# Thresholded attention feeding a leaky-ReLU layer pair: small threshold operations and some copies change engine, transposed weights change their PSUM banks and shape, and early loads change place

## The chip, the cores and the metric

The kernel runs on one core of one Trainium2 chip. The metric is device microseconds of one execution, taken as the median of several runs. The core has five engines that each work through their own list in order: PE (matrix multiply, with a list of weight loads beside it), DVE (VectorE), ACT (ScalarE), POOL (GpSimd) and SP, which here only issues DMAs. Engines wait for each other through semaphores.

## The reference

```
def _attn_ref(q, k, v, tau):                      # q, k, v: 8 batches, 8 heads, 576 positions, 64 wide
    scale = 1.0 / np.sqrt(q.shape[-1])
    scores = scale * np.matmul(q, k.transpose(0, 1, 3, 2))
    thresh = np.max(scores, axis=-1, keepdims=True) - tau          # tau = 0.02
    scores = np.where(scores >= thresh, scores, -1000000000.0)
    scores = scores - np.max(scores, axis=-1, keepdims=True)
    attn = np.exp(scores)
    attn = attn / (np.sum(attn, axis=-1, keepdims=True) + 1e-09)
    return np.matmul(attn, v)

def reference(...):
    x = attn_out.transpose(0, 2, 1, 3).reshape(4608, 512)
    h = x @ w_in                                  # w_in 512 x 2048
    g = np.maximum(0.01 * h, h)
    return g @ w_out                              # w_out 2048 x 512
```

## The kernel before

The work is a list of 144 steps, 18 for each of the 8 batches. A step has 128 query rows of two heads (a "pair" of heads, four pairs to a batch): first the 512 main positions as 16 steps (two blocks, four pairs, two halves `c`), then the 64 tail positions of all heads as two tail steps. The order of every engine's list is written out by hand: one loop over `n` (lines 479 to 516) emits, in this order, the parts of several steps at once.

For step `n` the parts are these. `scores` (L217) makes 12 matmuls into PSUM: q and k are each held as a high and a low fp16 half, and three products are summed. `copy_min` (L225) copies the scores from PSUM to `s` on DVE, negated and scaled, and accumulates the row minimum `mn`, once for each head. `threshold` (L231) adds tau to `mn` and gives `th`, a 128x2 tile; it is on POOL. `exps`, emitted one iteration later, runs on ACT: an exponential `e` for the first head (L253), and for the second head of a "steep" step a very steep Prelu against `th` (L249) and then the exponential with its sum (L250). A step is steep if `n` is below 12 or if nothing is transposed two iterations on. `weights` (L263) is the DVE counterpart: `w = (s <= th) * e` with its sum, for one head of a steep step and for both of another. `recip` (L269, DVE) and `widen` (L272, POOL) write the reciprocal of the sums into block 9 of `w`, so that it is transposed with the weights.

The transposed weights `wT` come from a DMA transpose on SP's queue (L280), except for the first eight steps (`early`), which are transposed on PE by `turn_w_pe` (L289), emitted two iterations after the step. It makes two groups of five transposes, each into a PSUM tile `wp`. Both tiles come from the ring with the tag `h`, which has two buffers. ACT copies the first group and DVE the second (L290). The second group holds block 9, so it needs `widen`. The ring `h` is shared with the tiles `tp` of the q and k transposes and with `hp` of the first layer. `pv` (L301) multiplies with v, and `evacuate` (L323, DVE) scales the result by the reciprocal and gives `x`.

q and k must be split and transposed first. The keys of batch 0 in order are k0, q0, the k tails, k1, q1, k2, q2, k3, q3 and the q tails. The first five are split by ACT and DVE (`split_now`, L158 and L159) and the others by three POOL operations each (`split_scale` L138, `split_high` L144, `split_low` L148). `turn` (L177) transposes a split key on PE in pieces of 64 columns, into `tp`; one copy (L188, or two of L180 for tails) brings it to `kT` or `qT`. This copy is on ACT unless the call names another engine. `turns_at`, `pool_at` and `loads_at` say which iteration emits which of these; the keys k2, q2, k3, q3 and the q tails are transposed in iterations 1, 2, 3, 4 and 8, and batch 1's from iteration 9 on.

The weights of the two layers are loaded as fp16 by DMAs on POOL's queue: four for `w_in` (L441), two after each of two early splits, and four for `w_out` (L444) in iterations 2 to 5. The other loads are on SP's queue, except q0 and q1 on ACT's. Once four pairs of a block are done, `layer1` (L344 on PE, Prelu L346 on ACT) and `layer2` (L357 on PE) are emitted, one unit of the first and two of the second to an iteration, which over a batch is just what the batch brings.

Iteration `n` thus puts on POOL: whatever `pool_at` holds, then `widen` of step `n-1`, then `threshold` of step `n`:

```
        for f in pool_at.get(n, []):
            f()
        if 1 <= n <= N:
            last = steps[n - 1]
            weights(last)
            ...                        # recip and widen of the last step
        if n < N:
            threshold(steps[n])
```

Of the kernel before, what the change touches and what calls it, by code (L numbers as in the profile page):

```python
# [10 lines left out]
FP16 = mybir.dt.float16  # L11
AX = mybir.AluOpType
# [26 lines left out]
def kernel(  # L39
# [10 lines left out]
    nc = tc.nc  # L50
# [4 lines left out]
    tau_f = float(tau)  # L55
# [4 lines left out]
    ps = ctx.enter_context(tc.tile_pool(name="ps", bufs=1, space=bass.MemoryType.PSUM))  # L60
# [3 lines left out]
    ident = sb.tile([128, 128], FP16, name="ident")  # L64
# [19 lines left out]
    def load_tails(b, which, eng=None):  # L84
        t = sb.tile([128, 2, 2, 64], FP32, tag="rawt", bufs=2, name="rawt")
        src = SRC[which][b, :, MAIN:S, :].rearrange("(u sh) p d -> u p sh d", u=2)
        for u in range(2):
            (eng or nc.sync).dma_start(out=t[ds(64 * u, 64), :, :, :].rearrange("p s h d -> p (s h) d"), in_=src[u])
        tails[b, which] = t
# [29 lines left out]
    def turned_of(b, which):  # L119
        if (b, which) not in turned:  # L120
            turned[b, which] = sb.tile([128, 2, NP, WIDE[which]], FP16, tag=f"{which}T", bufs=2, name=f"{which}T")
        return turned[b, which]
# [28 lines left out]
    def split_now(key):  # L151
        t = halves[key] = new_half()
        for i in range(2):
            if key[1] == "t":
                src, n = tails[key[0], key[2]][:, :, i, :], 2
            else:
                src, n = pair_of(*key)[:, i, :, :], 4
            nc.scalar.activation(out=t[:, 0, 0:n, i, :], in_=src, func=AF.Copy, bias=0.0, scale=64.0)  # L158
            nc.vector.scalar_tensor_tensor(out=t[:, 1, 0:n, i, :], in0=src, scalar=64.0, in1=t[:, 0, 0:n, i, :],  # L159
                                           op0=AX.mult, op1=AX.subtract)  # L160

    def turn(key, copy=None):
        copy = copy or nc.scalar.copy
        b, p, which = key
        dst, half = turned_of(b, which), halves.pop(key)
        n = 2 if p == "t" else 4
        c0 = 0 if which == "q" else 64
        if p == "t":
            c0 = MAIN if which == "q" else 0
            tp = ps.tile([128, 2, 2, 2, 64], FP16, tag="h", bufs=2, name="tp")  # L170
        else:
            tp = ps.tile([128, 2, 4, 128], FP16, tag="h", bufs=2, name="tp")
        for x in range(2):
            for t in range(n):
                for h in range(2):
                    o = tp[ds(64 * h, 64), x, :, t, :] if p == "t" else tp[ds(64 * h, 64), x, t, :]
                    nc.tensor.transpose(o, half[:, x, t, h, :], ident[:, :])  # L177
        if p == "t":
            for x in range(2):
                copy(out=dst[:, x, :, ds(c0, 64)], in_=tp[:, x, :, :, :].rearrange("d u s p -> d (u s) p"))  # L180
            if which == "k" and b:
                nc.gpsimd.tensor_copy(out=dst[:, :, :, 576:640], in_=dst[:, :, :, 0:64])
            elif which == "k":
                for x in range(2):
                    nc.vector.tensor_copy(out=dst[:, x, :, 576:640],
                                          in_=tp[:, x, :, :, :].rearrange("d u s p -> d (u s) p"))
        else:
            copy(out=dst[:, :, p, ds(c0, 512)], in_=tp[:, :, :, :].rearrange("d x t p -> d x (t p)"))  # L188
# [3 lines left out]
    steps = []  # L192
# [27 lines left out]
    def copy_min(st):  # L220

        st.mn = sb.tile([128, 2], FP32, tag="mn", bufs=3, name="mn")
        st.s = sb.tile([128, 2, 576], FP32, tag="s", bufs=2, name="s")
        for h in range(2):
            nc.vector.tensor_scalar(  # L225
                out=st.s[:, h, :].rearrange("p (a b) -> p a b", a=2), in0=st.sc[h][:, :, 0:288],
                scalar1=-1.0 / UNIT, scalar2=None, op0=AX.mult, op1=AX.min, accum_out=st.mn[:, h : h + 1])

    def threshold(st):
        st.th = sb.tile([128, 2], FP32, tag="th", bufs=3, name="th")  # L230
        nc.gpsimd.tensor_scalar(out=st.th[:, :], in0=st.mn[:, :], scalar1=1.0, scalar2=tau_f, op0=AX.mult, op1=AX.add)  # L231

    def exps(st):

# [32 lines left out]
    def recip(pr, c, n):  # L267
        pr.rec = sb.tile([128, 2, 2], FP32, tag="rec", bufs=2, name="rec")
        nc.vector.reciprocal(out=pr.rec[:, 0:n, :], in_=pr.sum[:, ds(c, n), :])  # L269
# [5 lines left out]
    def new_wt(pr):  # L275
        pr.wt = sb.tile([128, 2, 10, 128], FP16, tag="wT", bufs=4, name="wT")
# [6 lines left out]
    def turn_w_pe(pr, c):  # L283
        if c == 0:
            new_wt(pr)
        for half, copy in enumerate((nc.scalar.copy, nc.vector.tensor_copy)):
            wp = ps.tile([128, 5, 128], FP16, tag="h", bufs=2, name="wp")
            for i in range(5):
                nc.tensor.transpose(wp[:, i, :], pr.w[:, c, 5 * half + i, :], ident[:, :])  # L289
            copy(out=pr.wt[:, c, ds(5 * half, 5), :], in_=wp[:, :, :])  # L290

    def pv(st):
        st.pv = ps.tile([128, 4, 128], FP32, tag="pv", bufs=1, name="pv")
# [85 lines left out]
    loads_at, turns_at, pool_at = {}, {}, {}  # L379

    def at(d, n, f):
        d.setdefault(n, []).append(f)

    def units(b):
        u = [(b, p, w_) for p in range(NP) for w_ in "kq"]
        return u[:2] + [(b, "t", "k")] + u[2:] + [(b, "t", "q")]

    for b in range(1, B):
# [6 lines left out]
        for i, key in enumerate(units(b)):  # L395
            n_ = base + 4 + 18 * i // 10 if b > 1 else 9 + 3 * i // 2
# [19 lines left out]
    def load_pair(p, which, eng):  # L416
        if p % 2 == 0:
            raws[0, p // 2, which] = sb.tile([128, 4, 256], FP32, tag="raw", bufs=4, name="raw")
        eng.dma_start(out=raws[0, p // 2, which][:, ds(2 * (p % 2), 2), :],
                      in_=SRC[which][0, ds(2 * p, 2), 0:MAIN, :].rearrange("h (p t) d -> p h (t d)", t=4))  # L420
# [1 line left out]
    load_pair(0, "k", nc.sync)  # L422
    load_pair(0, "q", nc.scalar)
    load_tails(0, "k", nc.sync)
    load_pair(1, "q", nc.scalar)
    load_pair(1, "k", nc.sync)
    for p in (2, 3):
        load_pair(p, "k", nc.sync)
        load_pair(p, "q", nc.sync)
# [9 lines left out]
    def load_w(i):  # L439
        if i < 4:  # L440
            nc.gpsimd.dma_start(out=w_in16[:, i, :], in_=moe_w_in[ts(i, 128), :])  # L441
        else:
            j = i - 4
            nc.gpsimd.dma_start(out=w_out16[:, ds(4 * j, 4), :],  # L444
                                in_=moe_w_out[ds(512 * j, 512), :].rearrange("(j p) f -> p j f", p=128))

    for i in range(4):
        at(pool_at, 2 + i, lambda i=i: load_w(4 + i))

    def split_pool(key):  # L450
        split_scale(key)
        split_high(key)
        split_low(key)

    first = units(0)
# [4 lines left out]
    turn(first[2])  # L460
    for key in first[3:5]:
        split_now(key)
    for i, key in enumerate(first[5:7]):
        split_pool(key)
        load_w(2 * i)
        load_w(2 * i + 1)
    for n_, key in zip((0, 1, 6), first[7:]):
        at(pool_at, n_, lambda key=key: split_pool(key))
    at(turns_at, 0, lambda: turn(first[3]))
    at(turns_at, 0, lambda: turn(first[4], nc.vector.tensor_copy))  # L470
    for n_, key in zip((1, 2, 3, 4, 8), first[5:]):
        at(turns_at, n_, lambda key=key: turn(key))

    N = len(steps)
    for st in steps:
# [2 lines left out]
    n = 0  # L478
    while n < N + PV_LAG + 2 or l1q or l2q or stores:
        for f in loads_at.get(n, []):  # L480
            f()
        if 1 <= n <= N:
            exps(steps[n - 1])
        if n < N:
            scores(steps[n])
            copy_min(steps[n])
        if n - 1 in pv_at:
            evacuate(pv_at[n - 1], n)
        for f in pool_at.get(n, []):
            f()  # L490
        if 1 <= n <= N:
            last = steps[n - 1]
            weights(last)
            if last.early:
                recip(last.pair, last.c, 1)
                widen(last.pair, last.c, 1)
            elif last.tail or last.c == 1:
                recip(last.pair, 0, last.pair.n)
                widen(last.pair, 0, last.pair.n)
                turn_w(last.pair)  # L500
        if n < N:
            threshold(steps[n])
        while stores:
            store()
        if l1q and l1q[0][3] <= n:
            layer1()
        for f in turns_at.get(n, []):
            f()
        if 2 <= n < N + 2 and steps[n - 2].early:
            turn_w_pe(steps[n - 2].pair, steps[n - 2].c)  # L510
        for _ in range(2):
            if l2q:
                layer2()
        if n in pv_at:
            pv(pv_at[n])
        n += 1
# [33 lines left out]
```

## Time and profile before

| quantity | value |
|---|---|
| median of three runs | 531.41 us (530.39 to 531.99) |
| the profiled execution | 528.87 us, of which the span from first to last instruction is 527.1 us |
| busy share of the span: PE, DVE, ACT, POOL | 92%, 82%, 82%, 60% |
| PE busy from 160 to 475 us | 313.8 of 315 us |
| PE busy from 0 to 100 us | 70.7 of 100 us |
| start of the score copies of steps 0, 3, 8, 9, 13 and 19 (first L225 of the pair) | 12.65, 27.51, 45.10, 51.91, 62.55 and 84.65 us |
| mean granted TensorE clock | 0.983 |

The busy shares are averages over stages that differ. The last rows are the start of DVE's first score copy of a step, which serves as a clock of the loop: the first steps come slowly, and from about 160 us on PE is busy throughout. A span is measured from the first to the last instruction; the time of the profiled execution is 1.8 us longer.

### The profile page before, as it was taken

The page shows a single profiled execution, that of the slowest core. Times are in us where ns is not written, and L with a number is a line of the kernel's source. Part 1 is how long each engine was busy: PE and PEld are TensorE (multiplying, and loading weights), DVE is VectorE, ACT ScalarE, POOL GpSimd, SP SyncE. Part 2 cuts the span into 40 slices and gives each one's busy share as a digit, 9 for nine tenths or more (in the row PEclk, how much of TensorE's full clock was granted, in tenths as well). Part 3 has the DMA queues.
Part 4 walks back from the last instruction along what each step waited for, and adds up shares of the span by engine and source line. Part 5 has one row for each costly group of instructions (what it writes and reads, how often), then busy time and mean ns, then how long its engine had stood idle before and what let it go on. Part 6 is the DMA issues. An engine that isn't in the chain of part 4 may idle for free.

```text
span 527.1 us, 19148 instructions
## 1 busy us (share of the span) xinstructions
PE 487.0 (92%) x7824; PEld 343.5 (65%) x7824; DVE 432.7 (82%) x1182; ACT 431.3 (82%) x737; POOL 317.7 (60%) x559
## 2 busy tenths in 40 slices
PE   5586787998999999999999999999999999999995
PEld 3354565665766776676776676767767776667773
DVE  4577999999899988999899988998899988887100
ACT  4687967997889888988989888998989888999541
POOL 4946688766676767666777767676776763121000
PEclk9787999999999999999999999999999999999999
DMA  9992588499988999688989999889978997757511
GB/s 246 238 242 35 103 186 154 94 178 204 179 204 145 185 205 222 124 179 199 199 177 190 186 189 199 164 162 216 198 161 172 182 179 152 125 101 157 126 41 62
DMA packets 220696, 87.75 MB, mean 166 GB/s; under 512 B 190912, under 2 KB 217536, under 8 KB 220608
## 3 DMA queue, kind: packets, MB, share of 16 engines
q1 hardware_dynamic: 217376, 81.81, 76.7%
q0 software_dynamic: 2688, 4.19, 4.4%
q8 instruction: 61, 1.00, 0.8%
q10 hardware_dynamic: 544, 0.52, 0.3%
q14 instruction: 27, 0.22, 0.1%
HBM read 36.70 MB, written 9.44 MB: 88 GB/s over the span
## 4 chain that ended last, share of the span: by engine, by line
PE 66%; DVE 13%; POOL 7%; issue 6%; ACT 4%; DMA 3%; SPq 0%; POOLq 0%; DVEq 0%; ACTq 0%
PE hp L344 20%; PE o L357 18%; PE sc L217 17%; PE pv L301 6%; DVE w L263 6%; DVE s L225 6%; PE tp L177 4%; DMA wT<-w 2%; POOL half L148 2%; POOL scaled L138 1%; POOL half L144 1%; DMA rawt<-in_k_dram 1%; ACT s L249 1%; DVE x L323 1%; ACT e L253 1%
## 5 line engine op out<-in xcount | busy, mean ns | idle before, releaser
L225 DVE TENSOR_SCALAR_CACHE_REDUCE s<-sc 128x576 f32<-128x576 f32 x288 | 204.7, 748 | 32.1 <-PE sc L217 27.5
L263 DVE SCALAR_TENSOR_TENSOR w<-s,th,e 128x576 f16<-128x576 f32 x210 | 194.3, 948 | 5.1 <-POOL th L231 4.3
L253 ACT ACTIVATE e<-s,mn 128x576 f16<-128x576 f32 x210 | 155.8, 774 | 0.0
L357 PE MATMUL o<-wout,g 128*64 128x512 f16 x1152 | 147.5, 379 | 0.7 <-ACT osb L363 0.7
L217 PE MATMUL sc<-kT,qT 64*128 64x288 f16 (+1 forms) x1920 | 139.8, 289 | 7.8 <-DVE s L225 7.6
L344 PEld LDWEIGHTS <-win 128*64 128x64 f16 x2560 | 118.1, 110 | 32.9 <-issue 30.5
L344 PE MATMUL hp<-x,win 128*64 128x256 f16 x2048 | 136.0, 275 | 0.4 <-ACT g L346 0.3
L217 PEld LDWEIGHTS <-qT 64*128 64x128 f16 (+1 forms) x1920 | 79.0, 98 | 61.8 <-issue 47.2
L272 POOL CAST w<-rec 128x256 f16<-128x256 f32 (+1 forms) x84 | 30.8, 367 | 129.8 <-DVE rec L269 119.9
L346 ACT ACTIVATE g<-hp 128x512 f16<-128x512 f32 x144 | 84.0, 584 | 23.3 <-PE hp L344 23.1
L249 ACT ACTIVATE s<-s,th 128x576 f32<-128x576 f32 x78 | 60.4, 775 | 49.3 <-POOL th L231 49.3
L148 POOL TENSOR_TENSOR half<-scaled,half 128x512 f16<-128x512 f32 (+1 forms) x75 | 81.1, 1082 | 5.9
L357 PEld LDWEIGHTS <-g 128*64 128x64 f16 x1152 | 62.2, 110 | 31.3 <-issue 1.5
L250 ACT ACTIVATE w<-s,minus_tau 128x576 f16<-128x576 f32 x78 | 60.5, 775 | 2.5
L144 POOL CAST half<-scaled 128x512 f16<-128x512 f32 (+1 forms) x75 | 59.2, 790 | 4.8
L301 PE MATMUL pv<-wT,v 128*64 128x256 f16 (+1 forms) x960 | 54.4, 250 | 6.0 <-DVE xt L313 2.2
L301 PEld LDWEIGHTS <-v 128*64 128x64 f16 x960 | 41.3, 111 | 25.6 <-DVE xt L313 5.6
L177 PE MATMUL tp<-ident,half 128*64 128x128 f16 x1152 | 49.2, 228 | 9.2 <-ACT half L158 5.2
L138 POOL TENSOR_SCALAR scaled<-raw 128x512 f32<-128x512 f32 x60 | 49.8, 830 | 9.8 <-DVE qT L188 5.7
L231 POOL TENSOR_SCALAR th<-mn 128x2 f32<-128x2 f32 x144 | 40.8, 283 | 19.6 <-DVE s L225 4.5
L177 PEld LDWEIGHTS <-half 128*64 128x64 f16 x1152 | 42.4, 115 | 13.3 <-issue 6.6
L188 ACT COPY kT<-tp 128x1024 f16<-128x1024 f16 x32 | 32.2, 1007 | 3.6 <-PE tp L177 3.6
(37 smaller groups left out, 275.4 us busy)
## 6 DMA issues: line engine op xcount, KB each, us to landing
vraw<-in_v_dram SPq DMA_DIRECT2D x16, 512.0 KB, 5.4
out_dram<-osb SPq DMA_DIRECT2D x16, 512.0 KB, 4.2
raw<-in_k_dram SPq DMA_DIRECT2D x14, 512.0 KB, 5.1
raw<-in_q_dram SPq DMA_DIRECT2D x14, 512.0 KB, 4.7
win<-in_moe_w_in_dram POOLq DMA_DIRECT2D x4, 512.0 KB, 9.6
wout<-in_moe_w_out_dram POOLq DMA_DIRECT2D x4, 512.0 KB, 9.5
wT<-w SPq DMA_TRANSPOSE x76, 5.5
raw<-in_k_dram SPq DMA_DIRECT2D x4, 256.0 KB, 4.9
```

What stands on the lines that cost most here:

```text
L144: nc.gpsimd.tensor_copy(out=halves[key][:, 0, 0:n, :, :], in_=scaled[key][:, 0:n, :, :])
L148: nc.gpsimd.tensor_tensor(out=halves[key][:, 1, 0:n, :, :], in0=scaled.pop(key)[:, 0:n, :, :], in1=halves[key][:, 0, 0:n, :, :], op=AX.sub ...
L177: nc.tensor.transpose(o, half[:, x, t, h, :], ident[:, :])
L217: nc.tensor.matmul(out=o, lhsT=lhs, rhs=turned[st.b, "k"][rows, kx, pair, ds(key0, 288)], start=(i == 0), stop=(i == 2), skip_group_check= ...
L225: nc.vector.tensor_scalar(out=st.s[:, h, :].rearrange("p (a b) -> p a b", a=2), in0=st.sc[h][:, :, 0:288], scalar1=-1.0 / UNIT, scalar2=No ...
L249: nc.scalar.activation(out=z, in_=z, func=AF.Prelu, bias=st.th[:, h : h + 1], scale=-1.0, alpha=1e20)
L253: nc.scalar.activation(out=st.e[:, h, :], in_=st.s[:, h, :], func=AF.Exp, bias=st.mn[:, h : h + 1], scale=-1.0)
L263: nc.vector.scalar_tensor_tensor(out=st.w[h], in0=st.s[:, h, :], scalar=st.th[:, h : h + 1], in1=st.e[:, h, :], op0=AX.is_le, op1=AX.mult, ...
L301: nc.tensor.matmul(out=o, lhsT=v16[st.b % 2][:, st.p + u, blk, :], rhs=rhs, start=(i == 0), stop=(i == 4), skip_group_check=True)
L344: nc.tensor.matmul(out=hp[ds(64 * u2, 64), jj, :], lhsT=w_in16[:, i, ds(128 * j + 64 * u2, 64)], rhs=g.x[:, i, :], start=(i == 0), stop=(i ...
L346: nc.scalar.activation(out=g.g[:, ds(nj * u, nj), :], in_=hp[:, :, :], func=AF.Prelu, bias=0.0, scale=1.0, alpha=0.01)
L357: nc.tensor.matmul(out=g.o[ds(64 * u2, 64), :], lhsT=g.g[:, j, ds(128 * m + 64 * u2, 64)], rhs=w_out16[:, j, :], start=(j == 0), stop=(j = ...
```

## The change

- `threshold` of steps 0 to 13 is on DVE instead of POOL. It is also emitted earlier in the iteration, for all steps: after the first item of `pool_at` and before the other items, `weights`, `recip` and `widen`.
- `turn_w_pe` makes each 128-column transpose as two of 64 columns, and its first group goes to a buffer of the ring `o` (one buffer, the accumulator of the second layer) instead of `h`. The second group stays in `h`. The tile is widened to a bank; five of its eight blocks are used.
- The copies of batch 0's q2, q3 and q tails after their transposes go to DVE instead of ACT.
- The load of q1 moves from ACT's queue to SP's, behind k1. The four loads of `w_in` stand together behind both POOL splits, and the four of `w_out` come one iteration later.

```
     def threshold(st):
         st.th = sb.tile([128, 2], FP32, tag="th", bufs=3, name="th")
-        nc.gpsimd.tensor_scalar(out=st.th[:, :], in0=st.mn[:, :], scalar1=1.0, scalar2=tau_f, op0=AX.mult, op1=AX.add)
+        eng = nc.vector if st.n < 14 else nc.gpsimd
+        eng.tensor_scalar(out=st.th[:, :], in0=st.mn[:, :], scalar1=1.0, scalar2=tau_f, op0=AX.mult, op1=AX.add)
...
         for half, copy in enumerate((nc.scalar.copy, nc.vector.tensor_copy)):
-            wp = ps.tile([128, 5, 128], FP16, tag="h", bufs=2, name="wp")
+            wp = ps.tile([128, 8, 128], FP16, tag="oh"[half], bufs=1 + half, name="wp")
             for i in range(5):
-                nc.tensor.transpose(wp[:, i, :], pr.w[:, c, 5 * half + i, :], ident[:, :])
-            copy(out=pr.wt[:, c, ds(5 * half, 5), :], in_=wp[:, :, :])
+                for u in range(2):
+                    nc.tensor.transpose(wp[ds(64 * u, 64), i, :], pr.w[:, c, 5 * half + i, ds(64 * u, 64)],
+                                        ident[:, :])
+            copy(out=pr.wt[:, c, ds(5 * half, 5), :], in_=wp[:, 0:5, :])
...
-    load_pair(1, "q", nc.scalar)
     load_pair(1, "k", nc.sync)
+    load_pair(1, "q", nc.sync)
...
     for i in range(4):
-        at(pool_at, 2 + i, lambda i=i: load_w(4 + i))
+        at(pool_at, 3 + i, lambda i=i: load_w(4 + i))
...
-    for i, key in enumerate(first[5:7]):
+    for key in first[5:7]:
         split_pool(key)
-        load_w(2 * i)
-        load_w(2 * i + 1)
+    for i in range(4):
+        load_w(i)
...
     for n_, key in zip((1, 2, 3, 4, 8), first[5:]):
-        at(turns_at, n_, lambda key=key: turn(key))
+        at(turns_at, n_, lambda key=key: turn(key, nc.vector.tensor_copy if key[2] == "q" else None))
...
-        for f in pool_at.get(n, []):
+        todo = pool_at.get(n, [])
+        for f in todo[:1]:
+            f()
+        if n < N:
+            threshold(steps[n])
+        for f in todo[1:]:
             f()
...
-        if n < N:
-            threshold(steps[n])
```

## The prediction

> **What bounds the kernel now.** I read the page's busy shares first, then its slices, then busy time by stage, then the waits over the whole span, and last the timeline of the first 62 us.
>
> ```profile
> PE 487.0 (92%) x7824; PEld 343.5 (65%) x7824; DVE 432.7 (82%) x1182; ACT 431.3 (82%) x737; POOL 317.7 (60%) x559
> ...
> PEclk9787999999999999999999999999999999999999
> ```
>
> PE looks like the bound, but the share is a mean. The stages say where it is true. Columns: window, its length, then busy time of each engine with its number of instructions, granted clock, DMA share, GB/s.
>
> ```profile
> 12.60:20.90 8.30, 5.96 (x75) 3.81 (x72) 4.91 (x14) 3.46 (x6) 7.68 (x11) 1.00 1.12 237
> 20.90:27.50 6.60, 2.96 (x24) 1.79 (x25) 3.10 (x9) 6.26 (x10) 6.19 (x13) 0.51 1.06 259
> 27.50:45.10 17.60, 13.07 (x165) 9.03 (x167) 15.08 (x42) 14.65 (x26) 10.36 (x23) 0.89 0.97 185
> 45.10:62.50 17.40, 12.56 (x164) 8.39 (x164) 13.71 (x38) 15.14 (x28) 9.54 (x18) 0.81 0.21 39
> 62.50:84.60 22.10, 17.96 (x321) 14.18 (x322) 21.09 (x52) 17.94 (x31) 18.18 (x29) 1.00 0.93 183
> 84.60:100.00 15.40, 12.12 (x206) 8.03 (x200) 13.36 (x32) 11.55 (x20) 13.30 (x22) 1.00 0.58 118
> ...
> 160.00:475.00 315.00, 313.82 (x5184) 220.24 (x5180) 287.44 (x796) 278.68 (x476) 201.91 (x350) 1.00 0.90 176
> ```
>
> From 160 to 475 us PE is busy 99.6%, and each iteration brings as much layer work as it takes, so nothing is caught up there: the edit can pay only before. The start up to step 13 (62.55 us) is bound by no engine's work but by chains between them: in the rows from 27.5 to 62.5 us DVE and ACT are each busy 28.8 and 29.8 of 35.0 us. From 62.5 to 84.6 us DVE is full (21.1 of 22.1), and from 84.6 to 100 POOL and DVE are (13.3 and 13.4 of 15.4).
>
> The waits over the span (total us, times, longest) name the links, and the timeline shows the two worst places:
>
> ```profile
> ACT s L249 <- POOL th L231: 49.3, 40, 4.6
> DVE w L263 <- POOL th L231: 4.3, 5, 2.1
> PE wp L289 <- ACT kT L188: 4.1, 3, 3.0
> PE wp L289 <- ACT qT L188: 3.6, 2, 2.8
> PE wp L289 <- ACT qT L180: 2.2, 1, 2.2
> ```
>
> ```profile
> 18.86 0.19 POOL L231 TENSOR_SCALAR th<-mn 128x2 f32<-128x2 f32 x1
> 19.09 0.77 ACT L249 ACTIVATE s<-s,th 128x576 f32<-128x576 f32 x1 [4.62 <-POOL th L231]
> ...
> 25.23 0.69 PE L289 MATMUL wp<-ident,w 128*128 128x128 f16 x5 [2.83 <-ACT qT L188]
> ```
>
> ```profile
> 46.26 1.16 POOL L148 TENSOR_TENSOR half<-scaled,half 128x512 f16<-128x512 f32 x1
> 46.45 1.58 DVE L263 SCALAR_TENSOR_TENSOR w<-s,th,e 128x576 f16<-128x576 f32 x1
> ...
> 48.47 0.69 PE L289 MATMUL wp<-ident,w 128*128 128x128 f16 x5 [2.18 <-ACT qT L180]
> ...
> 51.91 0.76 DVE L225 TENSOR_SCALAR_CACHE_REDUCE s<-sc 128x576 f32<-128x576 f32 x1 [2.22 <-PE sc L217]
> ```
>
> Step 0's threshold is a 0.19 us operation whose input is ready at 14.08 us, but it stands behind 4.8 us of splits and load issues on POOL. ACT waits 4.62 us for it, its next copies come late, the `wp` tile waits for these copies to free a buffer of the ring `h`, and scores of step 3, behind that on PE, start only at 25.86 us. The third fence is the same at steps 8 and 9: a `wp` tile waits for the tail copy on ACT, and DVE idles 2.22 us for scores.
>
> **The change, stage by stage.** I replay the in-order lists with the durations of the trace.
>
> *Steps 0 to 3.* The new threshold of step 0 follows its copies on DVE (end 14.08 us), so Prelu and exponential (0.77 + 0.97 us with its read) run from about 14.5 to 16.25. The copy of k2 (1.0) ends at about 17.75 instead of 21.66. ACT's exponentials of step 1 end at 20.3 instead of 24.3, and q2's copy (0.68 us by the `qT` copies that DVE already makes, 0.99 on ACT) ends on DVE at about 21.5. The ring is then free. What is late next is POOL: `widen` of step 0 stands behind the splits of k2, q2, k3 and q3 (2.53, 2.8, 2.55 and 2.9 us with gaps) and the four `w_in` issues (2.46 in all); from 8.5 us that gives 21.7 against 22.01 before, only one threshold (0.27) less, because the change puts all four loads there too. So PE's second group ends at about 22.3, scores of step 3 (1.62 us at the clock 0.51 of that stage) run to 23.9, and DVE's copy of step 3 starts at about 23.95 instead of 27.51: **3.5 us** gained. If the landing of k2, issued one DMA (0.56 us) later behind q1, moves the POOL chain, 3.0; if widen is quicker, 4.2.
>
> *Steps 3 to 13.* Here the loop becomes DVE's, since the waits on ACT and PE are gone and DVE gets work. Its own busy time there is 15.08 + 13.71 = 28.8 us, which already holds `weights` operations stretched by POOL (mean 1.00 us against 0.81 when undisturbed). Added are 10 thresholds, q3's copy (0.68) and the tails' copy (0.5, by the two 0.25 us copies of the k tails). A 128x2 operation on DVE has no row; its neighbours are the read of an accumulator (0.08) and the 128x2 reciprocal (0.17, with about 0.1 of gap behind its wait). I take 0.25, between 0.08 and the row of a DVE operation held by POOL (1.58 - 0.81 = 0.77 more). So 28.8 + 2.5 + 1.2 + 0.5 of gaps = 33.0 us against 35.0. ACT loses the 0.99 of q3 and 0.62 of the tails: 28.2. Two engines at 94% and 80% do not mesh fully, so I keep 0.5 to 2.0, take **1.3**, and hold -3 (every threshold at 0.77 and more, with 28.8 + 7.7 + 1.2 + 0.5 = 38.2 against 35.0) and +3.7 (every one at 0.08) as ends. Behind the waiting threshold on DVE stand `weights`, `recip` and the `wp` copy, and then PE's `pv`.
>
> The Trainium skill, "SBUF — State Buffer", Who interferes with whom, speaks against this move: a tensor_scalar of VectorE in a two-port mode and a GpSimd instruction exclude each other for a whole instruction. The trace agrees for the two-input `weights` operation: 1.58 us beside a split on POOL, 0.81 alone. By the rule each threshold could wait for the rest of a POOL operation; an estimate from it, with POOL busy 57% of the stage and half an operation of 0.7 us to wait, is 0.2 us each, about what I took.
>
> *Steps 13 to 26, and after.* From step 14 on the threshold is POOL's again, but no longer behind `widen`, which waits for DVE's reciprocal. DVE waited for it three times after 62 us, 1.9 us in all (0.48, 0.59 and 0.84), with DVE or POOL full around. Step 13 adds 0.25 on DVE. POOL at 86% takes part of it back, so I count **1.0**, ends 0 and 1.7. The larger part of the 49.3 us of ACT's waits lies in the stage where PE is full: **0**, hidden by PE's work; if PE had gaps there, its 1.2 idle us in 315 are all there is.
>
> *The rest.* The transposes: 80 of 128 columns become 160 of 64. Five of the old take 0.45 us at full clock, and sixteen of `tp`, which have the new form, 0.64, so ten take 0.40: nothing, on an engine with 30% idle there. Between `wp` and its neighbours no gap of PE shows that would go with the shape. The first group's buffer `o` is not needed by layer 2 before about step 20. q1's copy waits for its load, now at 3.3 us on SP's queue; with 5.2 us to land it is there at 8.5 to 9, and ACT reaches it at 10.4; SP's other early loads issue some 0.5 us later, the nearest user being POOL's k2, priced above. The `w_in` loads land within 12 us, by 28, for a first use near 55; `w_out` is used from about 85 us. Both are hidden, and would cost at most their shift of 2 to 4 us if they were not.
>
> Sum: 3.5 + 1.3 + 1.0 = **5.8 us**. The profiled execution's 528.87 us (span 527.1) becomes 523.1; it lies 2.5 us under the median, and I take the same difference from 531.41: **525.6 us**.
>
> **The rivals.** *POOL holds DVE, slower.* Thresholds on DVE wait for the splits and casts beside them. For it: the 1.58 us row, and the late load issues that crowd POOL. Against: score copies from PSUM never stretch (0.75 us throughout), and what the threshold waits out, `weights` behind it need not. With 5.8 + 14 x 0.25 = 9.3 us gained before any threshold is paid, it decides from 0.66 us a threshold; at 0.9 it costs 12.6, a loss of 3.3: 534.7 us.
>
> *The start's gain is given back.* Batch 1's splits, with POOL at 82% and 86% in the two rows from 62.5, or DVE at 95%, set when the full stage begins, and the earlier start only waits there. For it: those shares. Against: those splits, too, begin earlier. If step 13's 4.8 us shrink to 0.8: 530.6, no change.
>
> *A fuller gain.* The lists mesh, thresholds are cheap: 4.2 + 3.7 + 1.7 = 9.6 us, 521.8.
>
> *It does not act.* If `widen` held PE at step 0 and each ring wait came back as another, only the 1.9 us of DVE's later waits would go: 529.5.
>
> **How the numbers follow.** The forecast case, 523.5 to 527.5 us, 0.55; the fuller gain 0.13; little acting, 528 to 529.8, 0.14; given back 0.09; slower by POOL 0.09. About 0.3% (1.6 us) is what a measurement of this kernel can tell from no change: faster 0.82, same 0.09, slower 0.09. The range runs from the fuller gain to the given-back case, 521.3 to 530.6.
>
> **What would show it.** Right: the wait of L249 for `th` absent before step 13; DVE's copy of step 3 near 24 us and of step 13 near 57.8; DVE above 90% busy from 24 to 58; PE's waits for ACT's copies at L289 gone, with the first waiting instead on `widen`; the stage from 160 us unchanged but some 6 us earlier. Wrong: step 3 early but step 13 not; thresholds on DVE well above 0.3 us; step 19 less ahead of its old 84.65 than step 13 of its 62.55.

## The result, and the profile after

The changed kernel took 523.0 us (median of four runs, 521.46 to 524.23) against 530.94 us for the kernel before: a ratio of 0.9847, 95% interval 0.9814 to 0.9879, or 7.9 us. In a later session it was 523.04 against 531.9 us (0.9842, 0.9816 to 0.9868). Forecast were 525.6 us, with a range of 521.3 to 530.6.

The profiled execution took 523.44 us. Its page, busy shares and granted clock:

```profile
PE 485.7 (93%) x7904; PEld 342.0 (66%) x7904; DVE 422.7 (81%) x1200; ACT 431.9 (83%) x733; POOL 331.5 (64%) x545
...
PEclk9899899999999999999999999999999999999999
```

Busy time by stage (columns as before). The first two rows run from step 3 to 13 and from 13 to 19, like two rows of the kernel before (27.5 to 62.5 and 62.5 to 84.6 us); the third runs on from step 19, and the last is the full stage, five us earlier:

```profile
24.70:57.10 32.40, 25.41 (x398) 17.63 (x400) 30.23 (x92) 28.59 (x50) 19.88 (x35) 0.89 0.75 144
57.10:77.20 20.10, 17.20 (x322) 13.71 (x324) 19.27 (x52) 18.20 (x30) 17.21 (x25) 1.00 0.85 178
77.20:93.00 15.80, 11.77 (x206) 7.80 (x202) 13.45 (x37) 10.87 (x18) 14.99 (x24) 1.00 0.63 128
155.00:470.00 315.00, 310.10 (x5124) 216.88 (x5122) 273.61 (x786) 277.24 (x472) 211.72 (x346) 1.00 0.85 174
```

From step 3 (24.7 us) to step 13 (57.1) DVE is busy 30.23 of 32.40 us, 93%: it now sets the pace there. But PE, which was busy 313.8 of 315 us in the full stage before, is busy 310.1. The chain at the start, from the timeline:

```profile
14.46 0.56 DVE L232 TENSOR_SCALAR th<-mn 128x2 f32<-128x2 f32 x1
...
15.05 0.78 ACT L250 ACTIVATE s<-s,th 128x576 f32<-128x576 f32 x1 [0.50 <-DVE th L232]
...
22.47 0.29 POOL L273 CAST w<-rec 128x128 f16<-128x128 f32 x1
...
22.81 0.32 PE L291 MATMUL wp<-ident,w 128*64 128x128 f16 x2 [2.98 <-POOL w L273]
...
24.71 0.76 DVE L225 TENSOR_SCALAR_CACHE_REDUCE s<-sc 128x576 f32<-128x576 f32 x1 [1.05 <-PE sc L217]
```

ACT's wait of 4.62 us is 0.50 us. What is late next is `widen` of step 0 on POOL, and PE's second group waits 2.98 us for it. The waits over the whole span (total, times, longest) show what took the place of the old ones:

```profile
POOL th L232 <- DVE s L225: 56.6, 65, 3.0
...
PE wp L291 <- POOL w L273: 4.0, 2, 3.0
PE pv L304 <- DMA wT<-w: 5.2, 6, 2.4
```

POOL now waits for DVE in its threshold, where ACT used to wait for POOL. PE waits more for transposed weights that come by DMA (1.6 us before, 5.2 now).

The clock of the loop, for all kernels that were run: start of the first score copy of steps 3 and 13, steps 13 to 34, steps 43 to 143 (all us, one profiled execution each), then the median time and the ratio to the kernel before.

| kernel | 3 | 13 | 13 to 34 | 43 to 143 | median | ratio (95%) |
|---|---|---|---|---|---|---|
| before | 27.51 | 62.55 | 73.26 | 320.0 | 530.94 | |
| before, again | 27.52 | 62.52 | 73.35 | 321.6 | (530.52, one run) | |
| changed | 24.71 | 57.13 | 70.09 | 324.5 | 523.0 | 0.9847 (0.9814 to 0.9879) |
| changed, again | 24.53 | 56.89 | 70.03 | 322.5 | 523.04 | 0.9842 (0.9816 to 0.9868) |
| threshold part alone (repeat) | 24.21 | 57.06 | 70.64 | 322.3 | 521.29 | 0.9798 (0.9771 to 0.9824) |
| all but the threshold part | 26.09 | 58.21 | 73.41 | 324.8 | 529.02 | 0.9934 (0.9912 to 0.9957) |
| changed, old place from step 14 | 25.32 | 56.78 | 73.67 | 324.2 | 526.87 | 0.9901 (0.9872 to 0.993) |
| changed, all thresholds on POOL | 25.60 | 59.06 | 70.44 | 323.4 | 522.67 | 0.9837 (0.9799 to 0.9875) |
| early place alone | 27.43 | 63.32 | 71.20 | 322.4 | 526.62 | 0.9912 (0.9889 to 0.9935) |
| ring alone | 24.81 | 58.15 | 73.19 | 321.3 | (525.67, one run) | |
| q copies alone | 27.13 | 62.49 | 75.15 | 321.3 | (532.01, one run) | |
| changed, w_in loads later | 22.26 | 54.46 | 70.51 | 323.9 | 521.81 | 0.9819 (0.9795 to 0.9843) |
| threshold part, w_in loads later | 23.67 | 57.09 | 71.13 | 323.2 | 522.95 | 0.9804 (0.9777 to 0.9831) |

The first three of these columns repeat from execution to execution within 0.3 us for the same kernel (two pairs). The kernel with the old place from step 14 on is the changed kernel up to step 13, yet its step 3 came 0.6 and 0.8 us later than in the two executions of that, so differences under 1 us at step 3 mean little. The fourth column does not repeat: 2.0 us lie between the two executions of the changed kernel.

### The profile page after: what moved, and what is told of

Same layout as the page of the kernel before. It is cut to its first block, busy times and chain, and to the rows that moved or that the text cites. A ratio compares the mean times of both kernels' runs of the same rounds, so it can differ in the third digit from the quotient of the medians.

```text
span 521.7 us, 19307 instructions
## 1 busy us (share of the span) xinstructions
PE 485.7 (93%) x7904; PEld 342.0 (66%) x7904; DVE 422.7 (81%) x1200; ACT 431.9 (83%) x733; POOL 331.5 (64%) x545
## 3 DMA queue, kind: packets, MB, share of 16 engines
q8 instruction: 62, 1.02, 0.8%
## 4 chain that ended last, share of the span: by engine, by line
PE 65%; DVE 16%; DMA 7%; ACT 6%; POOL 3%; issue 2%; DVEq 0%; POOLq 0%
PE hp L347 20%; PE o L360 18%; PE sc L217 17%; DVE s L225 8%; DMA wT<-w 7%; PE pv L304 6%; DVE w L264 5%; PE tp L177 4%; ACT e L254 1%; ACT s L250 1%; DVE x L326 1%; ACT kT L188 1%; DMA raw<-in_k_dram 1%; POOL half L148 1%; ACT osb L366 1%
## 5 line engine op out<-in xcount | busy, mean ns | idle before, releaser
L264 DVE SCALAR_TENSOR_TENSOR w<-s,th,e 128x576 f16<-128x576 f32 x210 | 177.2, 866 | 1.9 <-DMA wT<-w 1.7
L349 ACT ACTIVATE g<-hp 128x512 f16<-128x512 f32 x144 | 85.1, 591 | 58.8 <-PE hp L347 58.2
L232 POOL TENSOR_SCALAR th<-mn 128x2 f32<-128x2 f32 x130 | 54.9, 422 | 84.4 <-DVE s L225 56.6
L148 POOL TENSOR_TENSOR half<-scaled,half 128x512 f16<-128x512 f32 (+1 forms) x75 | 81.5, 1087 | 1.7
L144 POOL CAST half<-scaled 128x512 f16<-128x512 f32 (+1 forms) x75 | 62.5, 834 | 4.8 <-POOL th L232 0.2
L273 POOL CAST w<-rec 128x256 f16<-128x256 f32 (+1 forms) x84 | 32.0, 381 | 52.2 <-DVE rec L270 50.0
L138 POOL TENSOR_SCALAR scaled<-raw 128x512 f32<-128x512 f32 x60 | 48.3, 805 | 7.8 <-DMA raw<-in_k_dram 5.9
```

The costliest lines, as they stand in the source:

```text
L144: nc.gpsimd.tensor_copy(out=halves[key][:, 0, 0:n, :, :], in_=scaled[key][:, 0:n, :, :])
L148: nc.gpsimd.tensor_tensor(out=halves[key][:, 1, 0:n, :, :], in0=scaled.pop(key)[:, 0:n, :, :], in1=halves[key][:, 0, 0:n, :, :], op=AX.sub ...
L264: nc.vector.scalar_tensor_tensor(out=st.w[h], in0=st.s[:, h, :], scalar=st.th[:, h : h + 1], in1=st.e[:, h, :], op0=AX.is_le, op1=AX.mult, ...
L349: nc.scalar.activation(out=g.g[:, ds(nj * u, nj), :], in_=hp[:, :, :], func=AF.Prelu, bias=0.0, scale=1.0, alpha=0.01)
```

## The experiments

**The threshold part alone** (on the kernel before):

```
     def threshold(st):
-        nc.gpsimd.tensor_scalar(out=st.th[:, :], ...)
+        eng = nc.vector if st.n < 14 else nc.gpsimd
+        eng.tensor_scalar(out=st.th[:, :], ...)
...
-        for f in pool_at.get(n, []):
+        todo = pool_at.get(n, [])
+        for f in todo[:1]:
+            f()
+        if n < N:
+            threshold(steps[n])
+        for f in todo[1:]:
             f()
...
-        if n < N:
-            threshold(steps[n])
```

> The kernel before with one part of the change alone: the threshold earlier in the iteration for all steps, and on DVE for steps 0 to 13. Rings, transposes, copies and loads as before. Theory of the prediction (a chain: threshold, then ACT's copies, then the ring): step 0's threshold comes near 14.5 us instead of 18.86, the copy of k2 ends near 18, and the score copy of step 3 starts near 24.7 us, as in the changed kernel, because POOL's widen is next late whatever the ring does; later the copies on ACT keep the ring waits, step 13 near 59.5 us (57.1 changed, 62.55 before), time about 526.5 us. Rival (the ring is what matters): step 3 stays at 26.5 us or later, step 13 above 61 us, time above 529 us.

Median 522.64 us, ratio 0.980 (0.9764 to 0.9836, without the profiled execution). That one took 1643 us, with PE busy more than three times as long as in any other, so its steps say nothing, and the kernel was run again:

> The kernel before with the threshold part alone, repeated because its profiled execution was one in which PE ran about three times slower than in all others, so that its steps can't be read. Theory (threshold and ring stand in for each other at the start): step 3 near 25 us, step 13 at 57.5 to 59 us, steps 13 to 34 in 70 us, ratio 0.985. Rival (the threshold alone leaves the ring's waits): step 13 above 60 us, ratio 0.99. Second rival (thresholds on DVE alone are better than the whole change): step 13 below 57 us, ratio 0.980.

Ratio 0.9798, step 3 at 24.21, step 13 at 57.06 us. The start is that of the whole change to 0.1 us: with the threshold moved, ring, pairs, q copies and loads add nothing there. The timeline shows why:

```profile
20.85 0.38 PE L290 MATMUL wp<-ident,w 128*128 128x128 f16 x4 [1.62 <-ACT qT L188]
...
22.34 0.29 PE L290 MATMUL wp<-ident,w 128*128 128x128 f16 x1 [1.10 <-POOL w L273]
...
24.21 0.76 DVE L225 TENSOR_SCALAR_CACHE_REDUCE s<-sc 128x576 f32<-128x576 f32 x1 [1.06 <-PE sc L217]
```

The ring's wait for ACT's copy of q2 is still there, but it ends before POOL's `widen` does, so nothing depends on it.

**All but the threshold part** (the changed kernel with `threshold` as before):

```
-        eng = nc.vector if st.n < 14 else nc.gpsimd
-        eng.tensor_scalar(out=st.th[:, :], ...)
+        nc.gpsimd.tensor_scalar(out=st.th[:, :], ...)
...
+        if n < N:
+            threshold(steps[n])          # behind weights, recip and widen again
         while stores:
```

> The changed kernel with the threshold put back on POOL and behind widen for all steps; rings, 64-column pairs, q copies and loads stay changed. Theory of the prediction: ACT waits again about 4.5 us for step 0's threshold and then in each step, the score copy of step 3 starts near 25.8 us, step 13 near 60 us, time 527.5 to 529 us. Rival (the ring is what matters): step 3 near 24.7 us, step 13 near 58 us, time 523 to 525 us.

Step 3 at 26.09, step 13 at 58.21, steps 13 to 34 in 73.41, 529.02 us. Neither theory holds in full: the time is the one that the prediction's theory gave, but step 13 is the rival's. The other parts bring 4.3 of the 5.4 us of the start without any threshold, and then lose 3.3 us to the changed kernel in steps 13 to 34.

**The ring alone, and the q copies alone** (each on the kernel before) split these other parts:

```
-            wp = ps.tile([128, 5, 128], FP16, tag="h", bufs=2, name="wp")
+            wp = ps.tile([128, 5, 128], FP16, tag="oh"[half], bufs=1 + half, name="wp")
```

> The kernel before with one edit: the first group of the transposed weights in the ring o. Transposes of 128 columns, copies, thresholds and loads as before. The kernel with everything but the threshold part reached step 13 at 58.2 us. Theory (of its parts it is the ring that takes PE's waits for ACT's copies away): step 3 near 25.5 us, step 9 near 47.5 us, step 13 near 59 us. Rival (it is the q copies on DVE): step 3 above 27 us, step 13 above 61 us.

```
-        at(turns_at, n_, lambda key=key: turn(key))
+        at(turns_at, n_, lambda key=key: turn(key, nc.vector.tensor_copy if key[2] == "q" else None))
```

> The kernel before with one edit: the copies of batch 0's q2, q3 and q tails on DVE. Theory (the ring is the cause, and q2's copy on DVE waits behind a reciprocal that waits for ACT): step 3 still near 27.3 us, steps 8 to 9 in less than 5 us instead of 6.8 since the tails' copy no longer waits behind ACT's exponentials, step 13 near 60.5 us. Rival: step 13 below 59 us.

The ring alone reaches step 13 at 58.15 us, all that the kernel with all but the threshold reached (58.21). The q copies reach it at 62.49: nothing (and the steps from 13 to 34 took 1.9 us longer). The 1.8 us expected from step 8 to 9 did not come either (44.41 to 51.32 us). The prediction had put PE's wait of 2.18 us there down to the tails' copy on ACT. On DVE that copy comes no sooner: it stands behind a reciprocal and starts 3.1 us after step 8's first score copy, where on ACT it started 2.7 us after it. PE waits as long as before (here the profile puts the end of it down to ACT's copy of the first group):

```profile
47.46 0.17 DVE L269 RECIPROCAL rec<-sum 128x2 f32<-128x2 f32 x1
47.54 0.47 DVE L180 COPY qT<-tp 128x256 f16<-128x256 f16 x2
...
47.84 0.69 PE L289 MATMUL wp<-ident,w 128*128 128x128 f16 x5 [2.23 <-ACT wT L290]
```

In the kernel with the ring alone ACT is as late as before (the copy of q2, last line here, started at 24.19 us before), and PE no longer waits for it:

```profile
22.37 0.23 PE L289 MATMUL wp<-ident,w 128*128 128x128 f16 x1 [0.26 <-POOL w L272]
22.54 1.15 PE L217 MATMUL sc<-kT,qT 64*128 64x288 f16 x12
...
24.21 0.99 ACT L188 COPY qT<-tp 128x1024 f16<-128x1024 f16 x1
```

So the chain of the start, threshold to ACT to ring to PE, can be cut at either link (step 13 at 57.06 and 58.15 us), and cutting it twice pays once (57.13).

**The place of the threshold from step 14 on:**

```
-        if n < N:
+        if n < 14:
             threshold(steps[n])          # early place
...
+        if 14 <= n < N:
+            threshold(steps[n])          # old place, behind widen
         while stores:
```

> The changed kernel, but from step 14 on the threshold stands where it stood before, behind widen on POOL. Steps up to 13 are as changed, so step 13 should start near 57.1 us again. Theory of the prediction (the early place saves DVE's waits in steps 13 to 26, about 1.0 us): 1 us slower than the changed kernel. Rival (POOL's early threshold waits for DVE's score copies, 56.6 us in the trace, holds the splits behind it, and PE pays for it from 155 us on, where PE's idle time has grown from about 1.3 us to 3.9 us): PE idle from 155 to 470 us back under 2 us, 2 us faster than the changed kernel.

The rival fell: PE was idle 4.7 us between 155 and 470 us, as in the changed kernel (4.9), and the time rose by 3 to 4 us (ratios 0.9901 and 0.9847, medians 526.87 and 523.0). The theory had the sign right and the size too small: steps 13 to 34 took 73.67 us, as in the kernel before, instead of 70.09. Here is where that goes, DVE's `weights` in these steps (34 operations: busy us, mean ns, then idle us before them) in the kernel before, the changed kernel, and this one:

```profile
L263 DVE SCALAR_TENSOR_TENSOR w<-s,th,e 128x576 f16<-128x576 f32 x34 | 35.0, 1056 | 1.9 <-POOL th L231 1.9
```

```profile
L264 DVE SCALAR_TENSOR_TENSOR w<-s,th,e 128x576 f16<-128x576 f32 x34 | 30.6, 928 | 1.9 <-DMA wT<-w 1.7 <-POOL th L232 0.2
```

```profile
L264 DVE SCALAR_TENSOR_TENSOR w<-s,th,e 128x576 f16<-128x576 f32 x34 | 34.2, 1032 | 1.4 <-POOL th L232 1.4
```

The early place does not only take DVE's waits for the threshold away (1.9 to 0.2). It makes `weights` itself shorter, by 4.4 us in all. Against that stand a new wait of 1.7 us, put down to a weights transpose, 1.1 us more for scores, and 0.5 us for step 13's threshold, which is now DVE's: 1.7 + 4.4 - 1.7 - 1.1 - 0.5 = 2.8 of the 3.2 us gained. What makes `weights` shorter is in the last section.

**All thresholds on POOL, at the early place** (the changed kernel with `st.n < 0` for `st.n < 14`):

> The changed kernel with the threshold on POOL for all steps, at the new early place. Theory (it is POOL's queue ahead of the first thresholds, not only the place in the iteration, that holds ACT): step 0's threshold comes near 19 us behind three splits and four loads, step 3 near 25.8 us, then steps follow without the wait behind widen, step 13 near 59 us, time about 525 us. Rival (only the place behind widen matters): step 13 within 0.5 us of 57.1 us, time 523 us. Second rival (the threshold on DVE costs DVE more than it saves): step 13 earlier than 57.1 us, time below 522.5 us.

Step 3 at 25.60 and step 13 at 59.06 us, near the theory's 25.8 and 59: behind POOL's splits the first threshold came at 19.31 us, and thresholds on POOL cost 1.9 us of the start. The end does not show it; 522.67 us lies inside the spread of the changed kernel.

**The early place alone** (on the kernel before):

```
-        for f in pool_at.get(n, []):
+        todo = pool_at.get(n, [])
+        for f in todo[:1]:
+            f()
+        if n < N:
+            threshold(steps[n])
+        for f in todo[1:]:
             f()
...
-        if n < N:
-            threshold(steps[n])
```

> The kernel before with the threshold at the new early place, on POOL for all steps; nothing else changed. From the runs so far: the kernel without any threshold change reached step 13 at 58.2 us and the whole change at 57.1, against 62.55 before; and only kernels with the early place from step 14 on ran steps 13 to 34 in 70.1 to 70.4 us instead of 73.3 to 73.7. Theory (two separate gains: a start in which ring and threshold stand in for each other, and 3.2 us behind it from the place): step 13 near 61 us, because step 0's threshold still stands behind POOL's splits and the ring still waits for ACT, then 70.3 us to step 34, time 526 to 527.5 us. Rival (the place is everything): step 13 below 58.5 us, time 523 us or less.

526.62 us, but step 13 came at 63.32 us, not near 61: without the ring and without DVE the place does nothing for the start (62.55 before). Its gain is behind it: 2.1 us in steps 13 to 34. The medians differ by 5.3 us, which the profiled execution, the slowest of the six, does not show.

**The changed kernel again:**

> The changed kernel once more, for a comparison on one chip with the kernel that has the threshold part alone, which gave a ratio of 0.980 to the kernel before where the changed kernel gave 0.985. Theory (the two are equal within the spread of 2 to 3 us that executions show): ratios within 0.004 of each other. Rival (the other parts cost something once the threshold is moved): the changed kernel slower by 1 us or more again.

523.04 us against 521.29 for the threshold part alone on the same chip: 1.7 us, with intervals that just overlap (0.9816 to 0.9868 and 0.9771 to 0.9824). It looks as if the other parts cost something, but the two profiled executions can't say where: at step 43 they are within 0.2 us of each other (156.06 and 156.19 us), and at the end within 0.4 (521.80 and 521.44). This stays open.

**The loads of `w_in` later,** on the changed kernel and on the threshold part alone (there with `w_out` in iterations 4 to 7):

```
     for i in range(4):
-        load_w(i)
+        at(pool_at, 2 + i // 2, lambda i=i: load_w(i))
```

> The changed kernel with the four loads of w_in on POOL's queue in iterations 2 and 3, two to each, instead of in front of the splits of k3 and q3. Theory of the prediction (POOL's chain to the widen of step 0 is what is next late): that widen comes 2.4 us earlier, near 20.1 us, the score copy of step 3 starts near 22.9 us instead of 24.7, and the rest follows: step 13 near 55.6 us, time 1.5 us below the changed kernel. Rival (from step 3 on DVE's work sets the pace whatever the start): step 3 earlier, step 13 still near 57 us, same time. Second rival (loads meet the casts of v and the later widens on POOL): step 13 later than 57.1 us.

> The kernel before with the threshold part (early place, DVE for steps 0 to 13) and the four w_in loads in iterations 2 and 3, the four w_out loads in iterations 4 to 7; ring, transposes, copies and q1's load as before. The threshold part alone gave 521.3 us and step 13 at 57.1; the late loads on top of the changed kernel gave step 3 at 22.3 and step 13 at 54.5, of which 1.2 us reached the end. Theory (the two add, because the ring never waits once ACT has its thresholds): step 3 near 22.3 us, step 13 near 54.7, time about 520 us, the fastest of all. Rival (with the old ring, the copies on ACT are next late when widen comes earlier): step 13 above 56.5 us, time 521 us or more.

On the changed kernel the widen of step 0 came at 19.99 us, step 3 at 22.26 and step 13 at 54.46: the chain that the prediction named is confirmed. Against the repeat of the changed kernel the lead is 2.4 us at step 13, 2.0 at step 34 and 1.3 at step 43, so it outlives the stage in which DVE is full, though not whole. The medians differ by 1.2 us (521.81 and 523.04), with intervals that overlap, so what reaches the end is not settled. On the threshold part alone step 13 stayed at 57.09 us, as the rival said, and this line names the reason:

```profile
21.65 0.44 PE L290 MATMUL wp<-ident,w 128*128 128x128 f16 x5 [1.64 <-ACT qT L188]
```

With `widen` early it is again the old ring, waiting for ACT's copy, that is last. So the ring, with what came along with it, is worth nothing beside the threshold as long as POOL is late, and 2.6 us at step 13 once POOL is not. (The `w_out` loads stand one iteration later here than there; that was not tested apart.) No version is clearly ahead of the others at the end: against the kernel before, the threshold part alone has the ratio 0.9798, with later loads 0.9804, and the changed kernel with later loads 0.9819, all with intervals that overlap.

**The kernel before, again:**

> The kernel before, unchanged, for a second profiled execution: the one on hand took 528.87 us where the median is about 532. Theory (that execution was a lucky one in the full stage: steps 43 to 143 took 320.0 us in it, and 322.3 to 324.8 us in seven profiled executions of other kernels, with or without the threshold's new place): the same steps now take 322 us or more, PE waits for transposed weights there, and the start is as before (step 13 near 62.6 us). Rival (the changes make the full stage slower by 3 us): 320 us again.

```profile
155.00:470.00 315.00, 312.27 (x5184) 219.28 (x5180) 287.29 (x797) 277.71 (x472) 202.13 (x353) 1.00 0.89 176
```

The start repeats to 0.05 us. The full stage took 321.6 us, between the 320.0 of the first execution and the 322 expected; PE was idle 2.7 us there instead of 1.2. That execution (530.52 us) was still among the quicker ones of a kernel whose medians were 530.9 to 533.2 us. So part of the 4.5 us that the changed kernel's profile loses against the first one in steps 43 to 143 is the luck of two executions, and between 0.9 and 2.9 us by the repeats (322.5 and 324.5 against 321.6) may be more than that. The table has a hint: six executions of kernels with the 64-column pairs and q1's load on SP took 322.5 to 324.8 us there, with the threshold part or without, and the seven others 320.0 to 323.2 us. But the two groups overlap, and no run has either part alone. What the full stage really costs is left open.

## Why the prediction was right, point by point

- *Where the gain lies.* Right. By step 34 the changed kernel was 8.6 us ahead (135.81 against 127.22 us), and the way there was as described: ACT's wait for the threshold down from 4.62 to 0.50 us, `widen` on POOL next late, DVE 93% busy from step 3 on.
- *Steps 0 to 3: 3.5 us.* Measured 2.8. The replay put step 3 at 23.95 us and it came at 24.71, because `widen` came at 22.47 instead of 21.7: POOL began 0.2 us later, and the split of k3 took 3.1 us instead of 2.55, since its L148 was held by `weights` as in the rows of the last section (1.68 us instead of 1.16).
- *Steps 3 to 13: 1.3 us, ends -3 and 3.7.* Measured 2.6, twice the forecast but within its ends. The sum gave DVE 32.5 us of work and 0.5 of gaps; the trace has 30.2 us of work and 2.2 of gaps. The threshold was priced well, 0.293 us for these ten against 0.25; but `weights`, carried over at its old mean of 1.00 us, took 0.854, which is 1.5 us in ten. The remaining difference is overlap of DVE's rows, whose lengths add up to 6.3 us more than its busy time (5.1 before). Both rows are DVE's from 24.7 to 57.1 us (busy us, mean ns):

```profile
L264 DVE SCALAR_TENSOR_TENSOR w<-s,th,e 128x576 f16<-128x576 f32 x10 | 8.5, 854 | 0.0
...
L232 DVE TENSOR_SCALAR th<-mn 128x2 f32<-128x2 f32 x10 | 2.9, 293 | 0.2
```

- *Steps 13 to 26 and after: 1.0 us, ends 0 and 1.7.* This is the mis-sized term. It measured 2.2 by step 26 and 3.2 by step 34, outside its ends, because only DVE's waits were counted (1.9 us) and not what the place does to the length of `weights` (4.4 us).
- *The full stage: 0.* It was not gained, as said. In the profiled pair it took 4.5 us more from step 43 to 143 and so hid half of a lead of 9.0 us; the medians show 7.9 and 8.9 us. That this pair differs by 5.4 us, close to the sum of 5.8, is luck: the terms were too small by 2.8 us in all, and a loss that was not forecast took about as much away.
- *The rest: nothing.* True of the start: with ring, pairs, q copies and loads the kernel reached step 13 at 58.21 us, with the ring alone at 58.15. The pairs were not run by themselves. The Trainium skill, "TensorEngine Tiling (Array Packing)", Key Properties, says that changing the tiling mode drains TensorE; of a gain from the single shape of 64 columns nothing is seen in these two figures.
- *What the prediction did not see:* that ring and threshold stand in for each other. It counted one chain, which is right for the whole change; without the threshold part its theory expected step 13 near 60 us, and 58.2 came; with it alone it expected 59.5, and 57.06 came.
- *The rivals.* POOL holding DVE would have needed 0.66 us a threshold; the mean over 14 was 0.356, the longest 0.62. The giving back before the full stage did not happen: the lead grew from 5.4 us at step 13 to 8.6 at step 34.

## What to carry to other kernels

Look for a tiny operation that stands in one engine's list behind work that it does not need: here a 0.19 us threshold stood behind an operation that waits for another step's reciprocal, and its place alone was worth more in the stage where DVE was full (2.1 us) than at the start where its wait was longest (nothing). Where several waits form one chain, price the chain and not the links: cut once, the second cut may be free of effect until something else moves. And when executions of one kernel differ by 2 us in a stage, compare a clock of the loop step by step, not two spans.

## What the runs showed of the hardware

The threshold, a 128x2 operation on DVE, takes 0.16 to 0.17 us by itself and up to 0.62 us beside POOL in the changed kernel (1.02 us for step 0 in the threshold part alone, where a split of POOL ran from 13.82 to 14.97 us and the threshold from 13.97 to 14.99), and the hold goes both ways. Four rows of the changed kernel in the order of their starts:

```profile
20.15 0.61 POOL L144 CAST half<-scaled 128x512 f16<-128x512 f32 x1
20.17 0.62 DVE L232 TENSOR_SCALAR th<-mn 128x2 f32<-128x2 f32 x1
...
20.70 0.81 DVE L264 SCALAR_TENSOR_TENSOR w<-s,th,e 128x576 f16<-128x576 f32 x1
...
20.85 1.67 POOL L148 TENSOR_TENSOR half<-scaled,half 128x512 f16<-128x512 f32 x1
```

The threshold started behind POOL's cast and ended with it. Then `weights` started first, and POOL's split took 1.67 us where it takes 1.15 to 1.16 alone. That agrees, to within 0.15 us in these rows, with the Trainium skill, "SBUF — State Buffer", Who interferes with whom: whichever of the two starts first has the shared ports for its whole instruction.

The early place changes what DVE's `weights` meets. Of its 34 operations in steps 13 to 34, those held by an L148 split of POOL, running or started at most 0.05 us after them, were together 6.3 us longer than the undisturbed 0.81 us in the kernel before (11 operations), 2.0 us in the changed kernel (7), and 5.2 us with the old place (9). Those that started while POOL's threshold was running or held took 0.81 to 0.82 us every time; there were 3, 13 and 3 of them. So the meetings moved onto POOL's threshold, whose median over the changed kernel was 0.58 us against 0.19 before. These rows, with the place put back in one of the three kernels, account for nearly all of the 4.4 us.

One execution of the threshold part took 1643 us: PE was busy 1629.6 us of a span of 1641.7, with the granted clock shown as full (1.000). No other execution did so, and no cause was found.
